# Small changes around four places where TensorE waits, in a one-core gated-attention kernel

## The chip, the core and the metric

The kernel runs on one core of a Trainium2 chip. The core has five engines that run side by side and wait for one another by semaphores: TensorE (PE in the profile: matrix products; PEld is its loading of weights), VectorE (DVE), ScalarE (ACT), GpSimd (POOL) and SyncE (SP, which here only issues transfers). Every float here is 32 bits wide; the products run on fp32r operands.

The metric is the device time of one execution in microseconds (us), as the median of some runs. The changed kernel is measured in the same way against the kernel before.

## The reference

`x` has 2,048 rows of 640 values. There are 32 heads of 128 values, each with its own keys and values, and a window of the last 512 of 2,048 cached positions; the dense branch has 1,728 hidden values.

```python
W = min(4096, max(256, Sk // 4))                  # 512
xn = (x - mean(x)) / sqrt(var(x) + 1e-5)          # per row

q = heads(xn @ wq)
scores = q @ k[:, -W:].T * Dh ** -0.5
o = softmax(scores) @ v[:, -W:]
s = merge(o) @ wo

h = relu(xn @ w1 + b1)
y = (h * h) @ w2 + b2
out = x + s * (y * sigmoid(y))
```

## The kernel before

Nearly everything is a product on TensorE, and precision is kept by splitting: each operand is written as a high part `hi` (a rounded copy, made by ScalarE) and a low part `lo = value - hi` (made by VectorE or GpSimd), and `triple` issues three matmuls, hi·hi, hi·lo and lo·hi, in this order. One matmul is 128x128 weights against 512 columns. The rows of `x` are cut into four tiles of 512 rows, t = 0 to 3, and the kernel works with values transposed (features on the partitions).

The program has three stages, one behind the other on TensorE.

1. **First steps (0 to 108 us).** Tile 0 is normalised and its dense branch is computed, 14 steps of an "up" product (`up`, w1, tile name `ph`) and a "down" product (`down`, w2, `py`). Beside it VectorE prepares the mean and the inverse deviation of the tiles 1 and 2 (T1, T2): `ln_load` reads the rows, `ln_block` takes the statistics into a tile `mv`, `ln_root` makes the inverse root. `mv` has a row on each partition, but what is needed is one value per column. So `ln_rows` turns `mv` (128 partitions x 8 values) round with a transposing matmul into a PSUM bank (`pmv`), copies it to a tile `lr`, stores that in DRAM (`mv_d`) and reads it back spread over all partitions (`mr`). `ln_chunk` then normalises the transposed `x` with it (`xc`).
2. **The other tiles' dense branch (108 to 284 us).** The up products of T1 and T2 are done together for pairs of weight blocks, with seven products in place of eight (`w_first` to `w_third`; a Strassen-Winograd form). For each pair p the kernel makes sums of weight blocks (`w_sums`, tiles `ws`), splits them into hi and lo (`w_split(p, 0)` gives `wa`, `w_split(p, 1)` gives `ws`, `w_split(p, 2)` gives `wc` and `wl`), and adds products on VectorE: in `w_second` the sum `wy = wa + p5`, in `w_third` the sum `wx = wa + p5`. PSUM banks are few, so a product into the bank of `wa` must wait until such a sum has read it. Between these, `gate(0, ...)` finishes tile 0. Then 28 "down" steps m follow (`c_load` reads, `c_prep` splits into `ch` and `cw` two steps ahead, `c_down` multiplies), and `gate(T1, ...)` after step 13 applies the sigmoid, which on ScalarE needs another function table. Tile 3 (LATE) gets its statistics in stage 2 with the same `ln_rows`, ahead of the last pair.
3. **Attention (284 to 1,949 us).** 128 units i, one head on one tile each, of 54 matmuls: `s_mm` (scores, `s`), `q_mm` (queries of a unit two ahead, `pq`), `v_mm` (`o`) and `r_mm` (output projection, `r`). In the first units early up products of tile 3 (`early_up`, `eu`) fill the places that the later stages don't use yet. Queries use one PSUM bank: `q_hi` (ScalarE) and `q_lo` (VectorE) must read it before the next `q_mm` may write it.

In stages 1 and 2 the code's own order counts: the wrapper `Ordered` keeps what `pe`, `dve`, `act`, `pool` and `sp` issue in program order on each engine, while calls through `nc.` are placed by the scheduler. In stage 3 the order comes from a list: `at(when, f, ...)` gives each call a planned time in us from the stage's start (a unit is `PERIOD` = 12.4 of these), and the calls are issued sorted by it. `pe.addr_align` puts empty instructions between units so that code blocks of 256 instructions end at chosen places.

Constants lie in the pool `cpool` (`ident`, `b_sb` with 96 floats a partition, four tiles `SQ` of 32 floats a partition), which stands ahead of all pools of the left side. In the built program every tile of 512 bytes or more per partition starts at a multiple of 512 bytes, but for one of the constants; two calls of `pad` with 480 bytes see to that on the right side.

Of the kernel before, what the change touches and what calls it, by code (L numbers as in the profile page):

```python
# [8 lines left out]
F32 = mybir.dt.float32  # L9
F32R = mybir.dt.float32r  # L10
AF = mybir.ActivationFunctionType
# [3 lines left out]
P = 128  # L15
NT = 512
# [9 lines left out]
def kernel(  # L26
# [14 lines left out]
    nc = tc.nc  # L41
# [4 lines left out]
    NB = NT // P  # L46
# [3 lines left out]
    LATE = NTILE - 1  # L50
# [89 lines left out]
    LS = {}  # L140

    def ln_load(t):
        mv = xp.tile([P, 4, NB], F32, tag="mv", name=f"mv{t}")[:, :2, :]
        sc = xp.tile([P, 3, NB], F32, tag="sc", name=f"sc{t}")
        xn = []
        for b in range(NB):
            xb = ln_tile(t, b)
            r0 = t * NT + b * P
            nc.sync.dma_start(xb, x[r0 : r0 + P, :])
            xn.append(xb)  # L150
        LS[t] = mv, sc, xn

    def ln_block(t, b):
        mv, sc, xn = LS[t]
        st = xp.tile([P, 2, 6], F32, tag="st", name=f"st{t}_{b}", bufs=4)
        hd = D // 2
        for i in range(2):
            dve.bn_stats(st[:, i, :], xn[b][:, i * hd : (i + 1) * hd])
        dve.bn_aggr(mv[:, :, b], st)

    def ln_var(t):
        mv, sc, xn = LS[t]
# [12 lines left out]
        return mv  # L175

    def ln_rows(t, mv):
        pm = psx.tile([P, NT], F32, tag="x", name=f"pmv{t}")
        (pe if t == LATE else nc.tensor).transpose(pm[: 2 * NB, :P], mv.rearrange("p a b -> p (a b)"), ident)
        row = xp.tile([2 * NB, P], F32, tag="lr", name=f"lr{t}", bufs=1)  # L180
        nc.vector.tensor_copy(row, pm[: 2 * NB, :P])
        d = dpool.tile([2, NT], F32, name=f"mv_d{t}")
        nc.sync.dma_start(d.rearrange("a (b p) -> (a b) p", p=P), row)
        bc = []
        for i in range(2):
            m = (
                pa.tile([P, D], F32, tag="xb", name=f"mr{t}_{i}", bufs=NB)
                if t == T2
                else xp.tile([P, D], F32, tag="mr", name=f"mr{t}_{i}")
            )[:, :NT]  # L190
            nc.sync.dma_start(m, d[i : i + 1, :].to_broadcast([P, NT]))
            bc.append(m)
        return bc
# [53 lines left out]
        return [PRE[0, k] for k in range(2)]  # L247

    def ln_first():
        mv = xp.tile([P, 4, NB], F32, tag="mv", name="mv0")  # L250
        sc = xp.tile([P, 3, NB], F32, tag="sc", name="sc0")
        sts = [xp.tile([P, 2, 6], F32, tag="st", name=f"st0_{b}", bufs=4) for b in range(NB)]
        n = NB // 2
# [428 lines left out]
        b["p5"] = xp.tile([P, NT], F32, tag="p5", name=f"p5_{p}", bufs=2)  # L682
        act.activation(b["p5"], b["y"], AF.Copy)

    def w_second(p):
        b = PB[p]
        prod(p, 6, b["a"])
        dve.tensor_tensor(b["y"], b["a"], b["p5"], op=ALU.add)
        prod(p, 2, b["x"])
        rest(p, 0, 0, b["x"])  # L690
        up_end(T1, PAIRS[p][0], b["x"])
# [127 lines left out]
    B32 = 32  # L819
# [407 lines left out]
    up(T2, rp)  # L1227
    w_load(2)
    w_sums(1)
    w_split(1, 0)  # L1230
    w_fifth(0)
    w_second(0)
    gate(0, gate_tile, (3, 4))
    w_split(1, 1)
    w_split(1, 2)
    NP = len(PAIRS)
    for p in range(1, NP):
        more = p + 1 < NP
        if p + 2 < NP:
            w_load(p + 2)  # L1240
        w_first(p)
        w_seed(p)

        def prepare():
            if more:
                w_split(p + 1, 0)
                w_sums(p + 1)
            else:
                for k in range(2):
                    c_prep(0, k)  # L1250

        w_third(p - 1, prepare, lambda: w_fifth(p))
        if p == 1:
            ln_load(LATE)
        if p in (2, 3):
            spill(p - 1, XS[p - 1])
        if 1 <= p <= NB:
            ln_block(LATE, p - 1)
        if p == NB:
            ln_var(LATE)  # L1260
            LN[LATE] = ln_root(LATE)
        if p == NP - 2:
            for m in range(3):
                c_load(m)
        if p == NP - 1:
            LN[LATE] = ln_rows(LATE, LN[LATE])
        w_second(p)
        if more:
            w_split(p + 1, 1)
            w_split(p + 1, 2)  # L1270
    up(T2, FC - 1)
    w_third(NP - 1, lambda: c_prep(1, 0), lambda: c_prep(1, 1))
    xctx.close()
    bctx.close()
    for m in range(2 * FC):
        t, f = CS[m]
        for n in {OPEN + 2: (m + 3, m + 4), OPEN + 3: ()}.get(m, (m + 3,)):
            if n < 2 * FC:
                c_load(n)
        if m + 2 < 2 * FC:  # L1280
            for k in range(2):
                c_prep(m + 2, k)
        c, odd = divmod(m - 2, 2)
        if not odd:
            if 0 <= c < DC:
                ln_chunk(LATE, c)
                for k in range(2):
                    ln_split(LATE, c, k)
            if 0 < c <= DC:
                spill(LATE, XS[LATE], slice(c - 1, c))  # L1290
        if m == OPEN:
            pools["ep"] = ctx.enter_context(tc.tile_pool(name="early", bufs=1, side="right"))
            load_raw("q", 0, 0)
            load_raw("k", 0, 0)
            open_xT(0, 0)
            for i in range(2):
                load_xT(0, 0, i, slice(0, DC))
        if m == OPEN + 2:
            for kind in "qk":
                prep(kind, 0, 0, dve)  # L1300
                load_raw(kind, 0, 1)
            open_xT(0, 1)
            for i in range(2):
                load_xT(0, 1, i, slice(0, DC))
        if m == OPEN + 4:
            for kind in "qk":
                prep(kind, 0, 1, dve)
        if m == 2 * FC - 1:
            hctx.close()
            pools["psa"] = ctx.enter_context(  # L1310
                tc.tile_pool(name="psa", bufs=1, space=PSUM, side="right")
            )
            q_mm(0, range(DC))
            q_hi(0)
            q_lo(0)
        if m in LEAD_STEPS:
            pe.addr_align(BLOCK, lead_slot(m))
        c_down(m)
        if m == FC - 1:
            gate(T1, gate_tile)  # L1320
# [69 lines left out]
    for i in range(NU):  # L1390
        t0 = i * PERIOD

        def on(when, f, *a):
            at(t0 + when, f, *a)

        hf, g, t, h = units[i]
        for c in range(KC):
            on(0.68 * c, align, i, SLOTS[c])
            on(0.68 * c, s_mm, i, c)
        on(0.68 * KC - 0.6, align, i, SLOTS[KC])  # L1400
        qs = [(i + AHEAD, 3.45 if i % G and i > UPG else 4.3, 4.1)]
        if i == 0:
            qs = [(1, 2.8, 4.1), (2, 9.1, PERIOD - 5.2)]
        elif i < UPG:
            qs = [(i + 2, 4.9 if i == 3 else 4.2, 4.1)]
        for n, q_at, low in qs if i + AHEAD < NU else ():
            for c in range(DC):
                on(q_at + 0.68 * c, q_mm, n, (c,))
            on(q_at + 3.5, q_hi, n)
            on(q_at + low, q_lo, n)  # L1410
        for c in range(KC):
            on(0.8 + 0.68 * c, max_fold, i, c)
        on(3.95, gather, i, "m")
        on(4.1, row, i, "m")
        for c in range(KC):
            on(10.4 + 0.4 * c, shift, i, c)
        on(11.7, expo, i, 0)
        on(12.7, p_hi, i, 0)
        on(13.8, expo, i, 1)
        on(PERIOD + 4.0, p_hi, i, 1)  # L1420
        on(13.9, p_lo, i, 0)
        on(16.2, s_add, i)
        on(PERIOD + 6.2, s_fold, i)
        on(PERIOD + 8.0, gather, i, "s")
        on(PERIOD + 8.5, row, i, "s")
        on(18.6, p_lo, i, 1)
        for c in range(KC):
            on(PERIOD + 8.5 + 0.68 * c, v_mm, i, c)
        on(2 * PERIOD + 4.2, o_norm, i)
        on(2 * PERIOD + 4.9, o_hi, i)  # L1430
        on(2 * PERIOD + 5.5, o_lo, i)
        if i % G == G - 1:
            for d in range(DC):
                last = i == NU - G - 1
                if i < NU - 1:
                    for when, js in (R_AT_END if last else R_AT)[d]:
                        on(when, r_mm, i, d, js, (R_BANK_END if last else R_BANK)[d])
                    on(when + 0.68 * len(js), r_acc, i, d)
                if g == NG - 1 and hf == 0:
                    at((i + (3, 4, 5, 4, 5)[d] + (t and d in (0, 3, 4))) * PERIOD + 4.3, store_acc, t, d)  # L1440
                    w = (NU // 2 + 9 + 4 * (t * DC + d)) * PERIOD
                    for k, n in enumerate("sxg"):
                        at(w + k * PERIOD - 0.6, load_finish, n, 0, t, d)
                    at(w + 3 * PERIOD - 0.7, finish_gate, 0, t, d)
                    at(w + 3 * PERIOD - 0.7, finish, 0, t, d)
# [67 lines left out]
    at(z + 32.0, late_h)  # L1513
    for n, ((f, c), u) in enumerate(zip(EARLY, EARLY_IN)):
        if u >= 0:
            first = EARLY_IN[n - 2] < u or u == 3
            at(
                u * PERIOD + (6.3 if u == 0 else 3.4 if first else 8.2) + 0.01 * n,
                early_up,
# [63 lines left out]
```

## Time and profile before

| what | value |
|---|---|
| median of 3 runs | 1951.23 us (1951.10 to 1951.89) |
| the profiled execution's own time | 1951.11 us |
| its span, first to last instruction | 1949.3 us |
| TensorE | busy 1941.4 us, 8,576 matmuls |
| VectorE | busy 1599.3 us |
| ScalarE | busy 1242.6 us |
| GpSimd | busy 1346.5 us |
| mean granted TensorE clock | 1.000 |

Rows of a timeline read: start, duration, engine, line, operation, output<-inputs, shape, count; a bracket at the end says how long the engine was idle before it and who ended that. Nearly all rows have line 77, that of the recording wrapper, so work is told apart by tile names; the profile leaves buffer numbers out. A matmul's row shows when it starts and when its last result is out, 0.39 us later for one alone, and the next one starts before that; so the time a group takes on TensorE is read from its start to the next group's start, not from its duration. Idle time of VectorE, ScalarE or GpSimd costs nothing unless TensorE ends up waiting for it.

### The profile page before, as it was taken

What the parts mean: (1) busy time and instruction counts of PE and PEld (TensorE: products, weight loads), DVE (VectorE), ACT (ScalarE), POOL (GpSimd) and SP (SyncE); (2) the same over time, 40 slices, a digit from 0 to 9 for tenths busy, and PEclk for the clock granted to TensorE, in tenths of its full rate; (3) what the DMA queues carried; (4) which work ended last, traced back from release to release, by engine and by line L of the source; (5) the groups of instructions that cost most, each with busy time, mean ns of one, the idle gap of its engine ahead of it and who ended that gap; (6) DMA issues with size and microseconds to landing.
All of it is one profiled execution on the core that took longest, in us unless ns stands there. A gap on an engine that the chain in (4) does not pass through costs nothing.

```text
span 1949.3 us, 28584 instructions
## 1 busy us (share of the span) xinstructions
PE 1941.4 (100%) x8576; PEld 1605.5 (82%) x8576; DVE 1599.3 (82%) x2758; ACT 1242.6 (64%) x2150; POOL 1346.5 (69%) x727
## 2 busy tenths in 40 slices
PE   9999999999999999999999999999999999999998
PEld 7888888888888888888888888888888888888887
DVE  6864747788888888888888878888888888888864
ACT  5665536766666666666666676666666666666643
POOL 0022107888888888888888878888888888888841
PEclk9999999999999999999999999999999999999999
DMA  7557953323233222332335433333333333332353
GB/s 221 184 192 252 366 190 109 95 88 96 90 92 95 91 91 93 92 92 92 93 100 184 140 109 109 114 114 115 114 114 114 114 114 114 97 93 92 85 187 119
DMA packets 147639, 246.43 MB, mean 126 GB/s; under 512 B 25020, under 2 KB 47334, under 8 KB 146214
## 3 DMA queue, kind: packets, MB, share of 16 engines
q1 hardware_dynamic: 144774, 232.64, 38.5%
q0 software_dynamic: 2576, 11.80, 1.5%
q8 instruction: 77, 1.26, 0.2%
q14 instruction: 68, 0.56, 0.1%
q10 hardware_dynamic: 144, 0.16, 0.0%
HBM read 213.59 MB, written 30.95 MB: 125 GB/s over the span
## 4 chain that ended last, share of the span: by engine, by line
PE 99%; DMA 0%; DVE 0%; SPq 0%; issue 0%; ACT 0%
PE pq L77 22%; PE r L77 22%; PE o L77 18%; PE s L77 18%; PE py L77 7%; PE ph L77 3%; PE ly L77 2%; PE wa L77 2%; PE lu L77 2%; PE wy L77 1%; PE wx L77 1%; PE eu L77 1%; DMA xb<-in_x_dram 0%; DMA wr<-in_w_dram 0%; PE px L77 0%; SPq L77 0%
## 5 line engine op out<-in xcount | busy, mean ns | idle before, releaser
L77 POOL TENSOR_TENSOR pt<-e,pt 128x1024 fp32r<-128x1024 f32 x256 | 615.2, 2403 | 113.5 <-ACT pt L77 68.9
L77 PE MATMUL r<-ot,wo 128*128 128x512 f32 x1920 | 496.6, 389 | 0.0
L77 PE MATMUL pq<-ax,wq 128*128 128x512 f32 x1920 | 456.1, 389 | 0.0
L77 PEld LDWEIGHTS pq<-ax,wq 128*128 128x128 f32 x1920 | 360.4, 188 | 75.1 <-DVE q L77 0.4
L77 PEld LDWEIGHTS r<-ot,wo 128*128 128x128 f32 x1920 | 360.5, 188 | 74.8
L77 PE MATMUL o<-pt,wv 128*128 128x512 f32 x1536 | 369.0, 389 | 0.0
L77 PE MATMUL s<-q,wk 128*128 128x512 f32 x1536 | 368.9, 389 | 0.0
L77 DVE TRANSPOSE_TENSOR_REDUCE rdm<-s 128x16 f32<-128x512 f32 x512 | 346.9, 712 | 8.0 <-PE s L77 7.9
L77 ACT ACTIVATE e<-e 128x1024 f32<-128x1024 f32 x256 | 269.7, 1054 | 123.3 <-DVE e L77 83.2
L77 PEld LDWEIGHTS s<-q,wk 128*128 128x128 f32 x1536 | 288.4, 188 | 59.8
L77 PEld LDWEIGHTS o<-pt,wv 128*128 128x128 f32 x1536 | 288.3, 188 | 59.9 <-POOL pt L77 0.2
L77 DVE TENSOR_TENSOR e<-s,bm 128x512 f32<-128x512 f32 x512 | 312.3, 665 | 5.3 <-DMA bm<-m_d 4.3
L77 POOL TENSOR_TENSOR su<-e,e 128x1024 f32<-128x1024 f32 x128 | 308.8, 2412 | 0.0
L77 ACT ACTIVATE pt<-e 128x1024 fp32r<-128x1024 f32 x256 | 272.0, 1062 | 6.9
L77 DVE TENSOR_TENSOR acc<-r,acc 128x512 f32<-128x512 f32 x300 | 203.6, 679 | 12.7 <-PE r L77 12.4
L77 ACT ACTIVATE rdm<-rdm 32x64 f32<-32x64 f32 x384 | 97.7, 255 | 182.3 <-DVE rdm L77 179.2
L77 DVE TENSOR_TENSOR ot<-o,ot 128x512 fp32r<-128x512 f32 x128 | 88.6, 692 | 86.1 <-ACT ot L77 86.1
L77 DVE TRANSPOSE_TENSOR_REDUCE rds<-su 128x32 f32<-128x1024 f32 x128 | 158.3, 1237 | 0.3 <-POOL su L77 0.3
L77 ACT ACTIVATE q<-pq 128x512 fp32r<-128x512 f32 x128 | 76.8, 600 | 120.0 <-PE pq L77 120.0
L77 ACT ACTIVATE rds<-rds 32x32 f32<-32x32 f32 x384 | 89.7, 234 | 60.0 <-DVE rds L77 56.6
L77 POOL TENSOR_TENSOR wo<-or,wo 128x640 fp32r<-128x640 f32 x64 | 101.0, 1578 | 30.1 <-ACT wo L77 30.1
L77 POOL TENSOR_TENSOR wv<-vr,wv 128x512 fp32r<-128x512 f32 x64 | 83.2, 1300 | 53.6 <-ACT wv L77 53.6
(171 smaller groups left out, 2005.3 us busy)
## 6 DMA issues: line engine op xcount, KB each, us to landing
bm<-m_d SPq DMA_DIRECT2D x128, 256.0 KB, 3.2
bs<-s_d SPq DMA_DIRECT2D x128, 256.0 KB, 4.0
qr<-in_wq_dram SPq DMA_DIRECT2D x64, 320.0 KB, 4.7
or<-in_wo_dram SPq DMA_DIRECT2D x64, 320.0 KB, 4.6
kr<-in_kT_dram SPq DMA_DIRECT2D x64, 256.0 KB, 4.4
vr<-in_v_dram SPq DMA_DIRECT2D x64, 256.0 KB, 4.4
cw<-in_w_dram SPq DMA_DIRECT2D x26, 320.0 KB, 4.5
h_m<-r SPq DMA_DIRECT2D x26, 256.0 KB, 2.1
```

What stands on the lines that cost most here:

```text
L77: ins = method(*args, **kwargs)
```

## The change

Five edits:

- `ln_rows` turns `mv` round on VectorE: `mv` grows to 32 values a partition (the unused ones set to zero by GpSimd), and one VectorE transposition in blocks of 32x32 writes `lr`. This gives the 8 rows in four pieces of 32 columns, so `mv_d` is written with four transfers in place of one. Three transposing matmuls, three PSUM tiles and three copies go. For T2 VectorE's transposition and SP's transfers also come earlier in their queues, ahead of the loads of w1 and w2 for step 9.
- At step m = 6 ScalarE runs a sigmoid over one value, into a new tile `table` (one float a partition, in `cpool`).
- In unit 1 all four early up products stand ahead of the queries of unit 3 (`pq3`), which move from 4.2 to 5.6 of the unit, and `q_lo` from 4.1 to 6.4 behind them.
- The split of the second pair's `wa` comes behind the fifth product's copy (`p5`) and the sum `wy` of the first pair.
- The splits of the second pair's `ws`, `wc` and `wl` come behind the first pair's sum `wx`.

```diff
     def ln_load(t):
-        mv = xp.tile([P, 4, NB], F32, tag="mv", name=f"mv{t}")[:, :2, :]
+        mv = xp.tile([P, 32 // NB, NB], F32, tag="mv", name=f"mv{t}")
+        nc.gpsimd.memset(mv[:, 2:, :], 0.0)
...
     def ln_rows(t, mv):
-        pm = psx.tile([P, NT], F32, tag="x", name=f"pmv{t}")
-        (pe if t == LATE else nc.tensor).transpose(pm[: 2 * NB, :P], mv.rearrange("p a b -> p (a b)"), ident)
-        row = xp.tile([2 * NB, P], F32, tag="lr", name=f"lr{t}", bufs=1)
-        nc.vector.tensor_copy(row, pm[: 2 * NB, :P])
+        row = xp.tile([P, B32], F32, tag="lr", name=f"lr{t}", bufs=1)
+        nc.vector.transpose(row, mv.rearrange("p a b -> p (a b)"))
         d = dpool.tile([2, NT], F32, name=f"mv_d{t}")
-        nc.sync.dma_start(d.rearrange("a (b p) -> (a b) p", p=P), row)
+        to = d.rearrange("a (b p) -> (a b) p", p=P)
+        for g in range(0, P, B32):
+            nc.sync.dma_start(to[:, g : g + B32], row[g : g + 2 * NB, :])
...
-    def w_second(p):
+    def w_second(p, between=None):
         b = PB[p]
         prod(p, 6, b["a"])
         dve.tensor_tensor(b["y"], b["a"], b["p5"], op=ALU.add)
+        if between:
+            between()
         prod(p, 2, b["x"])
...
     w_sums(1)
-    w_split(1, 0)
     w_fifth(0)
-    w_second(0)
+    w_second(0, lambda: w_split(1, 0))
     gate(0, gate_tile, (3, 4))
-    w_split(1, 1)
-    w_split(1, 2)
...
         def prepare():
+            if p == 1:
+                w_split(1, 1)
+                w_split(1, 2)
             if more:
...
+    table = cpool.tile([P, 1], F32, name="table")
     for m in range(2 * FC):
         t, f = CS[m]
+        if m == 6:
+            act.activation(table, b2_sb[:, :1], AF.Sigmoid)
...
         elif i < UPG:
-            qs = [(i + 2, 4.9 if i == 3 else 4.2, 4.1)]
+            qs = [(i + 2, {1: 5.6, 3: 4.9}.get(i, 4.2), 6.4 if i == 1 else 4.1)]
...
-            first = EARLY_IN[n - 2] < u or u == 3
+            first = EARLY_IN[n - 2] < u or u in (1, 3)
```

The order of the built program shows it at three places. The first is VectorE's queue between the first two pairs of stage 2 (`ws1`, `wa1`, `wc1`, `wl1` belong to the second pair, the sums `wy0` and `wx0` to the first; a name ending in `_1_` and a number on the left is a lo part). Before:

```order
L77 TENSOR_TENSOR ws1_1_1277<-wp1_0_1124,ws1_0_1276 128x256
L77 TENSOR_TENSOR wa1_1_1283<-wp1_0_1124,wa1_0_1282 128x512
L77 TENSOR_TENSOR wy0_1248<-wa0_1241,p5_0_1292 128x512
L77 SCALAR_TENSOR_TENSOR sg_1314<-py0_3_368,b_sb_65,sg_1314 128x512
L77 SCALAR_TENSOR_TENSOR sg_1318<-py0_4_369,b_sb_65,sg_1318 128x512
L77 TENSOR_TENSOR ws1_1_1323<-ws1_0_1276,ws1_0_1322 128x512
L77 TENSOR_TENSOR ws1_1_1323<-ws1_1_1277,ws1_0_1322 128x512
L77 TENSOR_TENSOR wc1_1_1329<-wp1_1_1126,wc1_0_1328 128x256
L77 TENSOR_TENSOR wl1_1_1331<-wp1_0_1124,wl1_0_1330 128x128
L77 TENSOR_TENSOR wl1_1_1331<-wp1_1_1126,wl1_0_1330 128x128
L77 TENSOR_TENSOR wx0_1249<-wa0_1241,p5_0_1292 128x512
```

And after:

```order
L77 TENSOR_TENSOR ws1_1_1281<-wp1_0_1128,ws1_0_1280 128x256
L77 TENSOR_TENSOR wy0_1252<-wa0_1245,p5_0_1292 128x512
L77 TENSOR_TENSOR wa1_1_1302<-wp1_0_1128,wa1_0_1301 128x512
L77 SCALAR_TENSOR_TENSOR sg_1318<-py0_3_369,b_sb_65,sg_1318 128x512
L77 SCALAR_TENSOR_TENSOR sg_1322<-py0_4_370,b_sb_65,sg_1322 128x512
L77 TENSOR_TENSOR wx0_1253<-wa0_1245,p5_0_1292 128x512
L77 TENSOR_TENSOR ws1_1_1348<-ws1_0_1280,ws1_0_1347 128x512
L77 TENSOR_TENSOR ws1_1_1348<-ws1_1_1281,ws1_0_1347 128x512
L77 TENSOR_TENSOR wc1_1_1354<-wp1_1_1130,wc1_0_1353 128x256
```

The lo part of `wa1` has moved one place back, behind the sum `wy0`, and the sum `wx0` has moved ahead of the five lo parts of the second pair. On ScalarE the same two moves stand: the copy `p5` is ahead of the hi part of `wa1`, and the copy `wx1<-wa1` ahead of the hi parts of `ws1`, `wc1` and `wl1`.

The second place is ScalarE's queue in the "down" steps (`ch` and `cw` with a step's number are hi parts, `xT3` is a hi part of tile 3). Step 6 before:

```order
L77 ACTIVATE cw7_0_2142<-cw7_2098 128x640
L77 ACTIVATE ch8_0_2166<-ch8_2136 128x512
L77 ACTIVATE cw8_0_2170<-cw8_2134 128x640
L77 ACTIVATE xT3_0_2053<-xc3_2_2174 128x512
L77 ACTIVATE ch9_0_2202<-ch9_2164 128x512
```

Step 6 after; ahead of T1's gate (`sg<-py1`), where the `ACT_TABLE_LOAD` stood before, there is none any more, and the number of table loads stays at six:

```order
L77 ACTIVATE cw7_0_2149<-cw7_2105 128x640
L77 ACT_TABLE_LOAD
L77 ACTIVATE table_1987<-b_sb_65 128x1
L77 ACTIVATE ch8_0_2174<-ch8_2143 128x512
L77 ACTIVATE cw8_0_2178<-cw8_2141 128x640
L77 ACTIVATE xT3_0_2060<-xc3_2_2182 128x512
```

A table load and the one-value sigmoid have come between the hi parts of steps 7 and 8.

The third place is TensorE's queue in unit 1. The end of the early products and the start of the queries before:

```order
L77 MATMUL eu12_3056<-xT3_1_2054,w1s12_960 128x512
L77 MATMUL eu12_3056<-xT3_0_2053,w1s12_960 128x512
L77 MATMUL pq3_3075<-ax0_1_0_2722,wq0_1_0_2772 128x512
L77 MATMUL pq3_3075<-ax0_1_1_2723,wq0_1_0_2772 128x512
L77 MATMUL pq3_3075<-ax0_1_0_2722,wq0_1_1_2773 128x512
```

And after, with six more matmuls of `eu12` ahead; before, these six stood behind the fifteen of `pq3`:

```order
L77 MATMUL eu12_3064<-xT3_1_2061,w1s12_964 128x512
L77 MATMUL eu12_3064<-xT3_0_2060,w1s12_964 128x512 x2
L77 MATMUL eu12_3064<-xT3_1_2061,w1s12_964 128x512
L77 MATMUL eu12_3064<-xT3_0_2060,w1s12_964 128x512 x2
L77 MATMUL eu12_3064<-xT3_1_2061,w1s12_964 128x512
L77 MATMUL eu12_3064<-xT3_0_2060,w1s12_964 128x512
L77 MATMUL pq3_3092<-ax0_1_0_2730,wq0_1_0_2780 128x512
L77 MATMUL pq3_3092<-ax0_1_1_2731,wq0_1_0_2780 128x512
```

The queries of unit 3 now start six matmuls later and end where the early products ended.

Last, the tile `table` lengthens the pool of the constants by 32 bytes a partition, and `mv` and `lr` change the length of the pool that holds them. In the built program most tiles of the left side (the accumulators, `ot`, the attention tiles `e`, `pt`, `bm`, and all of stages 1 and 2 but what lies on the right) now start 32, 160 or 288 bytes behind a multiple of 512. Of the 8,573 matmuls left, 4,791 read at least one operand that starts 32 bytes off a multiple of 64; before there was none.

More of the change, by code (lines that the diff above doesn't have):

```diff
@@ L158, in ln_block @@
             dve.bn_stats(st[:, i, :], xn[b][:, i * hd : (i + 1) * hd])
-        dve.bn_aggr(mv[:, :, b], st)
+        dve.bn_aggr(mv[:, :2, b], st)
     def ln_var(t):
@@ L249, in ln_first @@
     def ln_first():
-        mv = xp.tile([P, 4, NB], F32, tag="mv", name="mv0")
+        mv = xp.tile([P, 32 // NB, NB], F32, tag="mv", name="mv0")
         sc = xp.tile([P, 3, NB], F32, tag="sc", name="sc0")
```

## The prediction

> **What bounds the kernel now.** I read the page first, for the busy times.
>
> ```profile
> span 1949.3 us, 28584 instructions
> PE 1941.4 (100%) x8576; PEld 1605.5 (82%) x8576; DVE 1599.3 (82%) x2758; ACT 1242.6 (64%) x2150; POOL 1346.5 (69%) x727
> ```
>
> TensorE is idle for 1949.3 - 1941.4 = 7.9 us in all, and no other engine comes near it. A faster engine beside it gains nothing by itself; only matmuls that go, or places where TensorE waits, can gain. So the next view is the chain in order of time, for the pace and for what breaks it.
>
> ```profile
> 190.54 46.47 PE py L77 x205
> 237.04 43.40 PE py L77 x190
> 280.44 3.40 PE pq L77 x15
> ```
>
> The first row gives 46.47 / 205 = 0.2267 us from matmul to matmul: 15 take 3.40 us, 6 take 1.36 us. The 395 matmuls of the first two rows should take 89.53 us and take 280.44 - 190.54 = 89.90, 0.37 us more, all of it at the seam between the two. I then went through TensorE's timeline for every group that takes longer than its count allows. Where the change edits, I find seven; each is priced below as the start of the next group, minus its own start, minus count x 0.2267.
>
> **The transposes.** The first two, for T1 and T2:
>
> ```profile
> 40.31 0.27 PE L179 MATMUL pmv<-ident,mv 128*8 128x128 f32 x1
> 40.34 3.65 PE L77 MATMUL ph<-xT,w1s 128*128 128x512 f32 x15
> 43.83 3.56 PE L77 MATMUL py<-h,w2s 128*128 128x512 f32 x15
> ...
> 54.03 0.27 PE L179 MATMUL pmv<-ident,mv 128*8 128x128 f32 x1
> 54.06 3.67 PE L77 MATMUL ph<-xT,w1s 128*128 128x512 f32 x15
> 57.57 3.56 PE L77 MATMUL py<-h,w2s 128*128 128x512 f32 x15
> ```
>
> 43.83 - 40.31 - 3.40 = 0.12 us, and 57.57 - 54.03 - 3.40 = 0.14 us. The third (LATE) I take at their mean: 0.39 us in all, which goes. What comes instead must stay hidden. For T1:
>
> ```profile
> 40.94 0.30 SPq L183 DMA_DIRECT2D mv_d<-lr  x1
> 42.18 0.80 SPq L191 DMA_DIRECT2D mr<-mv_d  x2
> ...
> mr<-mv_d SPq DMA_DIRECT2D x6, 256.0 KB, 4.4
> ...
> 50.93 1.41 DVE L77 TENSOR_TENSOR xc<-xc,mr 128x512 f32<-128x512 f32 x2
> ```
>
> Three more stores of 0.30 us each put 0.90 us ahead of the two reads and of the weight loads queued behind them on SP. The reads then start at 43.1 and land by 43.1 + 0.8 + 4.4 = 48.3, 2.6 us before `xc` uses them; VectorE in turn no longer waits for TensorE's `pmv`. For T2 and LATE SP reaches the stores earlier in its queue, before the loads of step 9 and between stores of `h_m`; 0.9 us again, with a whole step of 6.80 us (two groups of 15) before the steps that use those loads. GpSimd's three memsets stand where it has nothing else to do until stage 2. I cost all of this at 0; if the cover were gone, each place would cost at most its 0.9 us.
>
> **The sigmoid.** ScalarE and VectorE at that seam:
>
> ```profile
> 233.46 0.74 ACT L77 ACTIVATE cw<-cw 128x640 fp32r<-128x640 f32 x1 [2.14 <-issue]
> 234.22 1.28 ACT L77 ACT_TABLE_LOAD   x1
> 235.51 3.00 ACT L77 ACTIVATE sg<-py,b_sb 128x512 f32<-128x512 f32 x5
> ...
> 236.24 3.39 DVE L77 SCALAR_TENSOR_TENSOR sg<-py,b_sb,sg 128x512 f32<-128x512 f32 x5 [1.18 <-ACT sg L77]
> ```
>
> T2's first "down" product needs a PSUM bank that VectorE has finished reading, at 236.24 + 3.39 / 5 = 236.92; TensorE goes on at 237.04, and needs two more matmuls to find its pace. The bank's own sums are complete 12 matmuls before the step's end, at about 234.3, when ScalarE is done with `cw`; without the 1.28 us table load `sg` starts there, over a microsecond earlier, and the bank is free at about 235.8, ahead of TensorE. The 0.37 us goes, and nothing is late behind it, since the four other banks follow at 0.68 us (3.39 / 5), the pace of three matmuls. The load itself moves to step 6:
>
> ```profile
> 209.06 0.61 ACT L77 ACTIVATE ch<-ch 128x512 fp32r<-128x512 f32 x1
> ...
> 212.76 0.63 ACT L77 ACTIVATE xT<-xc 128x512 fp32r<-128x512 f32 x1 [2.36 <-DVE xc L77]
> ```
>
> It delays `ch8` and `cw8` (209.06 on) by some 1.5 us, and through VectorE's queue the next `xT`. Step 8 starts on TensorE after 115 matmuls, at 190.54 + 26.1 = 216.6. Now ScalarE is through with `ch8` at 209.7, and three more operations of 0.6 to 0.8 us follow on the two engines (211.9 at the latest), so some 3 us are left after the delay. Cost 0. SP's order changes there as well (a read of attention's `ax` ahead of those of step 13, which starts only at 190.54 + 12 x 3.40 + 2.27 = 233.6); cost 0, and rival (d) below if not.
>
> **The fourth Q.**
>
> ```profile
> 305.44 1.52 PE L77 MATMUL eu<-xT,w1s 128*128 128x512 f32 x6
> 306.99 3.70 PE L77 MATMUL pq<-ax,wq 128*128 128x512 f32 x15
> 310.52 1.52 PE L77 MATMUL eu<-xT,w1s 128*128 128x512 f32 x6
> ...
> 306.28 0.65 DVE L77 SCALAR_TENSOR_TENSOR q<-pq,q 128x512 fp32r<-128x512 f32 x1
> ```
>
> 310.52 - 305.44 = 5.08 us for 21 matmuls of 4.76 us: 0.32 us, because the query bank is free only when VectorE's `q` ends at 306.93. Six early products in between take 1.36 us, so `pq3` starts at 308.16, 1.2 us after the bank is free. 0.32 us goes. What could be late next is the other side: `pq3` now ends at 311.6, so its hi part comes after ScalarE's other preparations, and its lo part behind four shifts on VectorE:
>
> ```profile
> 312.81 2.43 DVE L77 TENSOR_TENSOR e<-s,bm 128x512 f32<-128x512 f32 x4
> ...
> 318.68 3.56 PE L77 MATMUL pq<-ax,wq 128*128 128x512 f32 x15
> ```
>
> The lo part thus ends at about 312.81 + 2.43 + 0.65 = 315.9, and the bank is asked for again at 318.68 - 0.32 = 318.4. 2.5 us are left; cost 0.
>
> **The second pair's splits.** Here the edit moves work in both directions.
>
> ```profile
> 117.44 0.61 ACT L77 ACTIVATE wa<-wp 128x512 fp32r<-128x512 f32 x1
> 118.08 0.60 ACT L77 ACTIVATE p<-wy 128x512 f32<-128x512 f32 x1
> ...
> 117.82 1.26 DVE L77 TENSOR_TENSOR ws<-wp,ws 128x256 f32<-128x256 f32 x1
> 119.00 0.68 DVE L77 TENSOR_TENSOR wa<-wp,wa 128x512 fp32r<-128x512 f32 x1
> 119.61 0.69 DVE L77 TENSOR_TENSOR wy<-wa,p 128x512 f32<-128x512 f32 x1
> ...
> 124.77 0.70 DVE L77 TENSOR_TENSOR wx<-wa,p 128x512 f32<-128x512 f32 x1
> ...
> 119.33 1.60 PE L77 MATMUL wa<-xT,wa 128*128 128x512 f32 x6
> 120.77 1.54 PE L77 MATMUL wa<-T,ws 128*128 128x512 f32 x6
> ...
> 124.19 1.52 PE L77 MATMUL wy<-T,ws 128*128 128x512 f32 x6
> 125.55 1.62 PE L77 MATMUL wa<-T,wc 128*128 128x512 f32 x6
> 127.01 0.84 PE L77 MATMUL wa<-xT,wl 128*128 128x512 f32 x3
> ```
>
> The fourth product's group takes 127.01 - 125.55 - 1.36 = 0.10 us too long: its bank waits for the sum `wx` (124.77 to 125.47). With that sum ahead of the lo parts it is done by about 123.7, and the 0.10 us goes. But the first product of pair 1 (119.33) already takes 120.77 - 119.33 - 1.36 = 0.08 us too long. Its third matmul, due at 119.78, needs the lo part of `wa1`, which ends at 119.68 and reaches TensorE hardly in time. After the change VectorE makes `wy` first, whose inputs are ready (`p` on ScalarE by 118.1), at 119.00; so the lo part starts at 119.61 and ends 0.61 us later than now, with nothing in between to take this up. The wait grows by 0.61 us. The bounds: -0.08 us if the lo part comes in time after all (the `ws` row of 1.26 us may be shorter in another execution), +1.30 us if one more operation like the sum `wy` (0.69 us) gets ahead of it. I take 0.61, which stands on the rows at that very place. The lo parts of `ws1` come later as well (ready by 124.4, needed by the third matmul of the group at 124.19 + 0.61, that is at 125.3): cost 0.
>
> **The sum.** -0.39 - 0.37 - 0.32 - 0.10 + 0.61 = -0.57 us. The profiled execution took 1951.11 us in all, so 1950.54; it lies 0.12 us under the median of the runs, 1951.23, against which the sum gives 1950.7. That is 0.03% less. A measurement of this kernel can tell about 0.2%, 3.9 us, from no change; so this is no change.
>
> **Where the tiles lie.** The 32 bytes of `table` move most tiles of the left side off multiples of 512 bytes. The trace of before has no such operand, so it has no price for it. What it can hit first is the start, where nothing hides a transfer:
>
> ```profile
> 0.75 1.81 SPq L77 DMA_DIRECT2D xb<-in_x_dram  x4
> 3.63 0.89 DVE L77 BATCH_NORM_STATS2 st<-xb 128x6 f32<-128x320 f32 x2 [2.58 <-DMA xb<-in_x_dram]
> ```
>
> From issue to use are 2.88 us. Between 0 and, say, an eighth of this (0.36 us) I take 0, because no row shows a cost; the upper end stays in the range. [...] Later transfers have the margins above.
>
> **Rivals.** (a) Engines read the moved tiles slower, and the kernel is slower. 4,791 of the 8,573 matmuls read a moved operand. This decides at 3.9 + 0.6 = 4.5 us, which is 0.94 ns a matmul, 0.4% of 226.7 ns. At 1 ns the time would be 1950.7 + 4.8 = 1955.5, at 3 ns 1965. For it: there is not one such matmul before. Against it: the pace of all groups is the same 0.2267 us, whatever the operands. Chance 7%. [...]
> (b) The edits don't do what they say: the freed places are taken by a next wait a little later (the sigmoid's banks, the query bank), only the transposes' 0.39 us goes, and `wa1` costs its 0.61: 1951.23 + 0.22 = 1951.5. Chance 15%.
> (c) The `wa1` wait doesn't come, all gains do: 1951.23 - 1.18 - 0.08 = 1950.0. Chance 14%.
> (d) A new wait of one to three microseconds at a place that I hold covered (stores ahead of loads on SP, `ax` ahead of step 13's operands): 1952 to 1954. Chance 8%.
> (e) Faster by over 3.9 us: it would need half of TensorE's 7.9 us of idle time, and the places that the edits touch hold 1.3 us in all, the transposes included. Chance 1%.
>
> The forecast itself has the other 55%: between 1950.3 and 1951.2. The range, 1949.8 to 1952.8, holds the forecast, (b), (c) and part of (d), and the 0.36 us of the start. Within 0.2% are the forecast, (b), (c) and (d): 92%; slower 7%; faster 1%.
>
> **What would show it.** In the changed profile there should be 8,573 matmuls, no `pmv`; the `ph` groups of steps 5 and 7 should follow their `py` without an extra 0.1 us. The 395 `py` should take 89.5 us. `pq3` should start right behind twelve `eu` and take 3.40 us to the next group. The first product of pair 1 should take about 2.05 us to the next group, with VectorE's lo part of `wa` ending at its third matmul. A group of 15 that lasts more than 3.41 us in stage 3 would show rival (a); an idle row of TensorE that ends at a DMA, rival (d).

## The result: 1.7% slower, nearly all of it in the pace of the matmuls

The changed kernel takes 1984.67 us (median of 4 runs, 1984.42 to 1985.26), the kernel before on the same chip 1951.56 us: a ratio of 1.017 [1.0157, 1.0182], 33.1 us more. The prediction said 1950.7 and at most 1952.8.

The page of the profile after, first lines:

```profile
span 1982.9 us, 28597 instructions
PE 1973.9 (100%) x8573; PEld 1604.6 (81%) x8573; DVE 1615.9 (81%) x2758; ACT 1244.8 (63%) x2151; POOL 1348.2 (68%) x730
```

TensorE does three matmuls fewer and is busy 32.5 us longer (1941.4 before); its idle time has grown by 1.1 us only (from 7.9 to 9.0). So new waits do not explain the time. The granted clock is 1.00 in both. The page's costliest groups tell where the 32.5 us are. Before:

```profile
L77 PE MATMUL r<-ot,wo 128*128 128x512 f32 x1920 | 496.6, 389 | 0.0
L77 PE MATMUL pq<-ax,wq 128*128 128x512 f32 x1920 | 456.1, 389 | 0.0
L77 PE MATMUL o<-pt,wv 128*128 128x512 f32 x1536 | 369.0, 389 | 0.0
L77 PE MATMUL s<-q,wk 128*128 128x512 f32 x1536 | 368.9, 389 | 0.0
```

After:

```profile
L77 PE MATMUL r<-ot,wo 128*128 128x512 f32 x1920 | 509.6, 396 | 0.0
L77 PE MATMUL pq<-ax,wq 128*128 128x512 f32 x1920 | 459.1, 390 | 0.0
L77 PE MATMUL o<-pt,wv 128*128 128x512 f32 x1536 | 379.0, 395 | 0.0
L77 PE MATMUL s<-q,wk 128*128 128x512 f32 x1536 | 373.7, 392 | 0.0
```

The first number behind the bar is the group's busy time, the second the mean duration of one matmul. The four groups of attention take 13.0 + 3.0 + 10.0 + 4.8 = 30.8 us more. Nothing waits longer there; each matmul is a little slower, and the groups are not equally slow. The timeline of TensorE in the steady part of attention, three rows of before and then the stretch after the change:

```profile
1007.57 2.88 PE L77 MATMUL o<-pt,wv 128*128 128x512 f32 x12
1010.28 1.52 PE L77 MATMUL r<-ot,wo 128*128 128x512 f32 x6
1011.64 1.52 PE L77 MATMUL s<-q,wk 128*128 128x512 f32 x6
```

```profile
1000.95 1.56 PE L77 MATMUL r<-ot,wo 128*128 128x512 f32 x6
1002.35 2.92 PE L77 MATMUL s<-q,wk 128*128 128x512 f32 x12
1005.11 0.86 PE L77 MATMUL r<-ot,wo 128*128 128x512 f32 x3
1005.81 3.59 PE L77 MATMUL pq<-ax,wq 128*128 128x512 f32 x15
1009.24 1.56 PE L77 MATMUL r<-ot,wo 128*128 128x512 f32 x6
```

Six r take 1002.35 - 1000.95 = 1.40 us, that is 233.3 ns each; before they took 1011.64 - 1010.28 = 1.36 us, 226.7 ns each. Fifteen pq take 3.43 us in place of 3.40. Taken over all matmuls of the trace, from start to next start, the mean went from 226.7 ns to 233.6 for r, 233.3 for o, 229.8 for s and 228.3 for pq.

Which groups are slow agrees with where their operands lie. For r and o the moving operand (`ot`, `pt`) has moved by 32 bytes and the weights (`wo`, `wv`, on the right side) have not; both are at 233. In stage 2, wx<-xT,wa has moved weights and an unmoved moving operand, and is at 233.3. But py<-h,w2s, where both operands have moved, is at 226.8 as before. Of the 8,516 large matmuls (those of 512 columns), 3,813 now have operands whose start places differ when taken modulo 256 bytes; before there was none. The groups s and pq have not moved at all and lose their time in the first five to eight matmuls behind an r or o.

### The profile page after: what moved, and what is told of

Its sections match the earlier page's. It is cut to its first block, busy times and chain, and to the rows that moved or that the text cites. A ratio compares the mean times of both kernels' runs of the same rounds, so it can differ in the third digit from the quotient of the medians.

```text
span 1982.9 us, 28597 instructions
## 1 busy us (share of the span) xinstructions
PE 1973.9 (100%) x8573; PEld 1604.6 (81%) x8573; DVE 1615.9 (81%) x2758; ACT 1244.8 (63%) x2151; POOL 1348.2 (68%) x730
## 3 DMA queue, kind: packets, MB, share of 16 engines
q1 hardware_dynamic: 144918, 232.65, 37.2%
## 4 chain that ended last, share of the span: by engine, by line
PE 98%; DVE 1%; ACT 0%; DMA 0%; issue 0%; SPq 0%; DVEq 0%
PE r L77 23%; PE pq L77 22%; PE o L77 18%; PE s L77 18%; PE py L77 7%; PE ly L77 2%; PE ph L77 2%; PE wa L77 2%; PE lu L77 2%; PE wy L77 1%; PE wx L77 1%; PE eu L77 1%; DVE T L77 0%; DVE ws L77 0%; DVE ts L77 0%; DMA wr<-in_w_dram 0%
## 5 line engine op out<-in xcount | busy, mean ns | idle before, releaser
L77 PE MATMUL r<-ot,wo 128*128 128x512 f32 x1920 | 509.6, 396 | 0.0
L77 PE MATMUL o<-pt,wv 128*128 128x512 f32 x1536 | 379.0, 395 | 0.0
L77 PE MATMUL s<-q,wk 128*128 128x512 f32 x1536 | 373.7, 392 | 0.0
L77 DVE TRANSPOSE_TENSOR_REDUCE rdm<-s 128x16 f32<-128x512 f32 x512 | 353.9, 716 | 10.5 <-PE s L77 10.1
```

Source lines behind the costliest of these rows:

```text
L77: ins = method(*args, **kwargs)
```

## The experiments

Theories first, by the letters that the expectations use. Q: the moved work costs the time (new waits, queues). O: every operand off its place costs by itself. M: what counts is that the two operands of a matmul start at different places, taken modulo some number of bytes. V: VectorE, ScalarE and GpSimd are slower on moved tiles, and TensorE suffers from that. A time below without a number of runs is that of one run; the runs of one kernel on one chip lie within 2.2 us of each other here.

**All five edits, tiles put back.** The changed kernel with the 32 bytes taken off another constant's tile, whose last floats nothing uses. All large products but 30 then have operands that agree modulo 256 bytes again; those 30, of `ph`, have weights 128 bytes off:

```diff
-    b_sb = cpool.tile([P, 96], F32, name="b_sb")
+    b_sb = cpool.tile([P, 88], F32, name="b_sb")
```

> The changed kernel with the tile of constants b_sb shortened from 96 to 88 floats a partition, which takes back the 32 bytes of table: every matmul operand starts at a multiple of 64 bytes again; all five edits stay. Theory M (a matmul is slow, by 6.7 to 7.0 ns, where its moving operand and its weights start at different places modulo 64 bytes): 226.7 ns from matmul to matmul everywhere, and only the five edits' own sum is left, 1951.6 - 0.6 = 1951.0 us. Theory O (any operand off a multiple of 64 is slow): the same 1951.0. Theory Q (the edits' own waits on TensorE leave it in a slow pace, the places of the tiles don't matter): 1984 to 1985.

Measured: 1950.55 us (11 runs) against 1951.56, a ratio of 0.9995 [0.9986, 1.0004]. The 33 us are gone although every edit is still there. Q falls.

**The 32 bytes alone.** The kernel before with that tile longer by 8 floats, and no other edit:

```diff
-    b_sb = cpool.tile([P, 96], F32, name="b_sb")
+    b_sb = cpool.tile([P, 104], F32, name="b_sb")
```

> The kernel before with b_sb lengthened from 96 to 104 floats, 32 bytes a partition, and nothing else: the left side's tiles move by 32 bytes as in the changed kernel, none of the five edits is there. Theories M and O: as slow as the changed kernel and 0.6 us more, since the edits' gain is missing: 1985.2 us. Theory Q: 1951.6.

Measured: 1985.18 us. The shift alone makes the whole slowdown.

**The same with 64 bytes** (112 floats).

> The kernel before with b_sb lengthened by 64 bytes: the left side's tiles move off their multiples of 512, but stay at multiples of 64. Theory M with a period of 64 bytes, and O: 1951.6 us, no change. If the multiple of 512 counts, or of 128: as slow as with 32 bytes, 1985 us. Theory Q: 1951.6.

Measured: 1978.36 us, 26.8 more than before. M with a period of 64 bytes falls, and so does O with multiples of 64: 64 bytes are not a harmless distance. The branch that foresaw the slowness of 32 bytes misses too, since this kernel is 6.8 us faster than that one. The timeline of this kernel:

```profile
1000.16 2.93 PE L77 MATMUL s<-q,wk 128*128 128x512 f32 x12
1002.93 0.86 PE L77 MATMUL r<-ot,wo 128*128 128x512 f32 x3
1003.63 3.61 PE L77 MATMUL pq<-ax,wq 128*128 128x512 f32 x15
1007.08 1.55 PE L77 MATMUL r<-ot,wo 128*128 128x512 f32 x6
1008.47 2.91 PE L77 MATMUL o<-pt,wv 128*128 128x512 f32 x12
1011.22 1.08 PE L77 MATMUL r<-ot,wo 128*128 128x512 f32 x4
```

Twelve o, with operands 64 bytes apart, take 2.75 us, 229 ns each, and twelve s, with both operands in place, 2.77 us, 231 ns each. The matmuls behind a change from one kind of group to the other settle slowly: the s at 1000.16 follow each other at 234, 231, 233, 236, 224, 231, 236, 228, 232, 231 ns and only then at 227.

**Only one operand of one group.** The kernel before, with the attention outputs 32 bytes later in slots that have room behind them:

```diff
-        OT[i] = [two[:, k, :NT] for k in range(2)]
+        OT[i] = [two[:, k, 8 : 8 + NT] for k in range(2)]
```

> The kernel before with the two halves of ot used from their 8th float on (32 bytes further inside the same tile), which moves the moving operand of the 1,920 r matmuls alone. Theories M and O: r goes from 226.7 to about 233.6 ns, 13.4 us, and the matmuls behind an r group (s, pq) take part of the 7.8 us that they lost in the changed kernel, 3 to 4: 1965 to 1969 us; o stays at 226.7. Theory Q: 1951.6.

Measured: 1974.17 us, 22.6 more. The mechanism is as expected, the size is not: r takes 13.2 us more (509.8 us busy), and the unmoved s, o and pq, at 228.2 to 228.6 ns, take the rest, 8.9 us. I had put 3 to 4 us on s and pq and nothing on o.

**Everything off, but equally.** This tells M from O and V: the changed kernel with an unused tile of 224 bytes at the top of the right side, which puts that side at 32 bytes too.

```diff
+    top = ctx.enter_context(tc.tile_pool(name="top", bufs=1, side="right"))
+    top.tile([P, 56], F32, name="top")
     xr = xctx.enter_context(tc.tile_pool(name="mxr", bufs=1, side="right"))
```

> The changed kernel with every tile of the right side moved by 32 bytes too, so that in all but 30 of the large products both operands start 32 bytes behind a multiple of 256. Theory M (what counts is the difference between the start places of the moving operand and of the weights, taken modulo 256 bytes): all groups go back to 226.7 ns a matmul, time 1950.5 to 1951. Theory O (every operand that does not start at a multiple of 256 bytes costs by itself): now all 8,573 matmuls have two such operands, time 1985 or more. Theory V (other engines are slower on moved tiles, and TensorE suffers from that): 1985 or more as well, since no tile of theirs has come back.

Measured: 1951.31 us (10 runs) against 1951.83, a ratio of 0.9997 [0.9988, 1.0007]. The page's groups of this kernel:

```profile
L77 PE MATMUL r<-ot,wo 128*128 128x512 f32 x1920 | 496.6, 389 | 0.0
L77 PE MATMUL pq<-ax,wq 128*128 128x512 f32 x1920 | 456.0, 389 | 0.0
L77 PE MATMUL o<-pt,wv 128*128 128x512 f32 x1536 | 369.3, 389 | 0.1
L77 PE MATMUL s<-q,wk 128*128 128x512 f32 x1536 | 369.1, 389 | 0.0
```

All groups are back at 389 ns, with 8,486 matmuls that read two operands off their places, and VectorE, ScalarE and GpSimd still working on moved tiles. O and V fall, M stands. VectorE's busy time says the same: it is 1615.9 us in the changed kernel and 1597.2 here, so it follows TensorE's pace and does not set it.

**The period and the grain.** The one line of `ot` again, with 1, 4, 16, 32, 48 and 64 floats in place of 8.

> The kernel before with the two halves of each attention output tile starting at the 2nd float of their slots, 4 bytes later; it is the moving operand of 1,920 products r. Theory M, with every difference counted in bytes: r at about 233 ns a matmul and the products behind it slower for some steps, as with 32 bytes, time 1965 to 1975. Theory M with a grain of 16 or 32 bytes: 4 bytes don't count, time 1951.5, r at 226.7 ns.

> The kernel before with the attention output tiles 16 bytes later in their slots. If the pace falls off with the difference of the two start places (236.0 ns at 4 bytes, 233.8 at 32), r takes 234 to 236 ns a matmul and the time is 1974 to 1985. [...]

> The same with 64 bytes: r at 229 to 231 ns (o had 228.9 and r 231.1 where both stood 64 bytes off their weights), 1,920 x 2.3 to 4.4 ns plus some steps of the products behind, time 1956 to 1965. If only the distance to the next multiple of 256 counted in one direction, falling from 4 to 128 bytes, r would be between 232.0 and 233.8 ns, time 1968 to 1974.

> The same with 128 bytes (the 33rd float). Theory M with a period of 256 bytes: r at about 231.7 ns, the mean of the few products of other kernels here whose operands differ by 128 bytes; 1,920 x 5.0 ns = 9.6 us and some steps of the products behind, time 1961 to 1970. With a period of 128 bytes: 1951.5, r at 226.7 ns.

> The same with 192 bytes, that is 64 bytes ahead of the next multiple of 256. If the sign of the difference counts (products with weights 64 bytes behind the moving operand took 233.4 ns, with the moving operand 64 bytes behind the weights 228.9), r is at 233 to 234 ns, time 1970 to 1976. If only its size counts, r is as with 64 bytes.

> The same with 256 bytes (the 65th float). Theory M with a period of 256 bytes: r at 226.7 ns, time 1951.5. With a period of 512 bytes or none: r slower than 228 ns, time 1960 or more.

Measured, with the mean of r from start to next start, and the range of the three other groups' means:

| `ot` later by | time, us | over before | r, ns | s, o, pq, ns |
|---|---|---|---|---|
| 4 bytes | 1985.40 | +33.6 | 236.0 | 229.3 to 230.2 |
| 16 bytes | 1972.36 | +20.4 | 231.2 | 228.6 to 229.7 |
| 32 bytes | 1974.17 | +22.6 | 233.8 | 228.2 to 228.6 |
| 64 bytes | 1980.45 | +28.5 | 232.2 | 229.9 to 230.7 |
| 128 bytes | 1968.43 | +16.6 | 232.0 | 227.9 to 228.3 |
| 192 bytes | 1971.27 | +19.3 | 233.3 | 227.9 to 228.3 |
| 256 bytes | 1951.32 | -0.5 | 226.7 | 226.7 |

The view of the instructions of `r` shows the two ends: shortest, median and longest duration in ns. With 4 bytes, and with 256:

```profile
L77 PE MATMUL r<-ot,wo x1920: 395/398/405, 337.6 to 1917.7; 128*128 128x512 f32 x192
```

```profile
L77 PE MATMUL r<-ot,wo x1920: 389/389/397, 337.1 to 1883.7; 128*128 128x512 f32 x192
```

The period is 256 bytes: 256 bytes cost nothing (-0.5 us), 128 do (16.6 us). No distance tried between 4 and 192 bytes is free, and the loss does not fall or rise with the distance. Three expectations missed. At 4 bytes I expected r at about 233 ns and at most 1975 us; it is the dearest distance, with 236.0 ns and 1985.40 us. At 16 bytes I weighed a fall of the pace with the distance, with r at 234 to 236 ns; it is at 231.2, faster than at 32 bytes. Below 16 bytes only 4 were run, so no grain is shown. At 64 bytes I expected r at 229 to 231 ns and at most 1965 us; r is at 232.2, and the settling of s, o and pq (3 to 4 ns on each of 4,992 matmuls) made it 1980.

The 192 bytes came out as expected, with r at 233.3 ns. With 64 bytes and with 192, which is 64 ahead of the next multiple of 256, the same kernel loses 28.5 and 19.3 us: the sign of the difference does count.

**Own weights, or the next ones?** While a matmul runs, the weights of the next one are loaded: in the trace of before a load lasts 188 ns and starts 0.22 us ahead of its own matmul, when the matmul before it has just started. N: the columns of the running matmul collide with that load. S: a matmul's columns stand against its own weights. The lo halves of `ot` and of `wo` are moved by 4 bytes, both and each alone:

```diff
-        OT[i] = [two[:, k, :NT] for k in range(2)]
+        OT[i] = [two[:, k, k : k + NT] for k in range(2)]
...
+        if tag == "wo":
+            o = name.startswith("wo")
+            two = [
+                pools["eo"].tile([P, D + 64 * i], F32R, tag=f"wo{i}", name=f"{name}_{i}", bufs=bufs)
+                for i in range(2)
+            ]
+            return [two[0], two[1][:, o : o + D]]
```

> The kernel before with the lo half of each attention output (ot) and the lo half of wo both 4 bytes later, the hi halves in place. A triple is hi with hi, lo with hi, hi with lo (ot first). Theory N (what collides is the reading of a product's columns and the loading of the next product's weights): the lo half of ot streams while the lo half of wo is loaded, both 4 bytes off, and the hi halves stream while hi halves are loaded, so every pair agrees: time 1951.5, r at 226.7 ns. Theory S (what counts is a product's columns against its own weights): two of the three products of each triple differ by 4 bytes, 1,280 in all; with 236.0 ns for them and slow steps in the other groups the time is 1968 to 1985.

> Control: only the lo half of ot 4 bytes later. By N and by S alike one product of each triple differs, 640 in all, and the time is 1957 to 1975. If it stays at 1951.5, one product in three is too few to matter, and the run with both lo halves moved cannot tell N from S by its time.

> Second control: only the lo half of wo 4 bytes later. By N the second product of a triple (the lo half of ot streams in place while the moved lo half of wo is loaded) collides, by S the third; either way 640 in all, and 1957 to 1975.

Measured: 1971.38, 1964.30 and 1970.97 us, against 1951.26 before. N as stated falls: with both halves moved every moving operand agrees with the weights loaded beside it, and 20.1 us are lost. The times lie where S has them. But S is not the whole of it: two differing products in three (20.1 us) cost no more than the one with `wo` alone (19.7), and in that run the second product of a group, whose own operands agree, already takes 235 ns on average, while the moved weights of the third are loaded. N and S at once would order the three times: they hit the second and third product of a triple in the first run, the second alone in the second run, and the second and third again in the last one. But the third product of a group takes only 228 ns there, so this is not shown either. Which two accesses collide stays open. The weight loads themselves last 188 ns in all these runs, as before.

**The edits without one of them.** The first experiment's kernel, with the split of the second pair's `wa` back where it was:

```diff
-    w_fifth(0)
-    w_second(0, lambda: w_split(1, 0))
+    w_split(1, 0)
+    w_fifth(0)
+    w_second(0)
```

> The changed kernel with all tiles back in place (as in the run with 88 floats in b_sb) and with the split of the second pair's wa back where it was before the change; the other edits stay. The wait at the first product of pair 1, 0.63 us in that run, should go back to the 0.08 us of before: 0.55 us less than that run, 1950.0, and 1.5 us under the kernel before. If the wait moves to the fourth product or to the sum wy, it stays at 1950.5.

Measured: 1950.05 us (11 runs) against 1951.97, a ratio of 0.9990 [0.9981, 0.9999]. It is the fastest kernel of this study, by a margin that is at the edge of what can be told. The product in question, in the first experiment's kernel and then in this one:

```profile
118.96 0.61 PE L77 MATMUL wa<-xT,wa 128*128 128x512 f32 x2
119.94 1.20 PE L77 MATMUL wa<-xT,wa 128*128 128x512 f32 x4 [0.36 <-DVE wa L77]
120.97 1.53 PE L77 MATMUL wa<-T,ws 128*128 128x512 f32 x6
```

```profile
119.11 1.56 PE L77 MATMUL wa<-xT,wa 128*128 128x512 f32 x6
120.51 1.53 PE L77 MATMUL wa<-T,ws 128*128 128x512 f32 x6
```

With the edit the six matmuls take 2.01 us, 0.65 over 1.36; without it 1.40.

## Why the prediction was wrong

**The step that failed** is "Where the tiles lie", and with it rival (a). I priced the new operand places at 0 for all but the start, gave rival (a) 7%, and held against it that "the pace of all groups is the same 0.2267 us, whatever the operands". That was no evidence: in the trace of before all 8,516 large matmuls had operands that agree modulo 256 bytes, so the one thing that the shift changes did not vary there. An equal pace over groups that are alike in this says nothing about groups that are not. The profile could not give the price, 30.8 us in attention; only a run could. The range should have reached for that rival, since nothing of before bounded it.

The rival's own form was wrong in three ways. It counted 4,791 matmuls that read a moved operand; what counts are the 3,813 whose two operands differ, and the 957 large ones whose operands lie off together keep the pace of before where they stand among themselves (py<-h,w2s, 226.8 ns). At 1 or 3 ns a matmul it was also priced too low: r alone has 6.9. And it left out the neighbours: s and pq, with no moved operand, lose 4.8 and 3.0 us of the 30.8. The sign that the prediction named for it did come: fifteen pq take 3.43 us in stage 3, over its 3.41.

The runs with `ot` alone moved show what a distance costs: 32 bytes cost r 7.1 ns a matmul, 16 bytes 4.5, and of the distances run only 256 bytes cost nothing. The measurement decides.

**The start.** The transfers into moved places were priced at 0 and bounded by 0.36 us, at the first block of x. No run shows that bound, an eighth of the 2.88 us from issue to use; in its place stand the times of the two profiles. That block comes no later: VectorE's first row with it starts at 3.59 us after, at 3.63 before. But the first large matmul starts at 12.17 us after, at 11.69 before:

```profile
11.69 1.63 PE L77 MATMUL ph<-xT,w1s 128*128 128x512 f32 x6
```

```profile
12.17 1.64 PE L77 MATMUL ph<-xT,w1s 128*128 128x512 f32 x6
```

These 0.48 us come from the third block, for which VectorE waits after, and did not before:

```profile
6.03 0.49 DVE L77 BATCH_NORM_STATS2 st<-xb 128x6 f32<-128x320 f32 x1
```

```profile
6.52 0.49 DVE L77 BATCH_NORM_STATS2 st<-xb 128x6 f32<-128x320 f32 x1 [0.54 <-DMA xb<-in_x_dram]
```

That the places cause this is not shown. The first large matmul starts at 11.77 to 12.17 us (12.02 on average) in the four kernels whose blocks of x lie 32, 64 or 160 bytes behind a multiple of 256: after, 32 and 64 bytes alone, everything off equally. It starts at 11.55 to 11.97 (11.73 on average) in the eleven with blocks at a multiple of 256. The averages differ by 0.3 us, within the bound, and the ranges overlap; the 0.48 us of the two executions above lie over it. In the first experiment and in the kernel with `wa` back the blocks lie 128 bytes behind such a multiple, and the matmul starts at 11.54 and 11.67, among the earliest. So in these two executions a start 128 bytes off a multiple of 256 did not make the matmul late.

Later transfers are not visibly slower: the main queue's packets take 37.2% of 16 engines' 1982.9 us, less than the 38.5% of 1949.3 us before.

**The five edits.** The sum was -0.57 us. The first experiment, where they stand alone, measures -1.0 us with an interval of -2.7 to +0.8, which cannot settle it; the rows of its trace can:

| term | predicted | in the first experiment |
|---|---|---|
| three transposes | -0.39 | -0.36: 3.41, 3.40 and 1.37 us to the next group in place of 3.52, 3.54 and 1.48 |
| sigmoid | -0.37 | gone: no step over 227 ns at that seam |
| fourth Q | -0.32 | gone: twelve eu in 2.72 us, fifteen pq in 3.40 |
| fourth product | -0.10 | gone: 1.36 us |
| `wa1` | +0.61 | 0.65 in place of 0.08: +0.57 |

The sums agree within 0.1 us. The 30 `ph` products with operands 128 bytes apart, which take 232.3 ns each, add 0.17 us that belong to the places and not to the edits. And the kernel with the split of `wa` back in its place loses the `wa1` term as worked out: 0.04 us too long where it was 0.65. The seam of the sigmoid is seen in the changed kernel's chain too; before, the 395 matmuls took 89.90 us:

```profile
192.69 89.54 PE py L77 x395
```

No new wait of rival (d)'s size came, and none of the freed places was taken by a next one, as rival (b) had it. (One group of twelve o is 0.17 us too long in the first experiment; in the kernel with `wa` back it is not.) Each of the prediction's five terms was right to a tenth of a microsecond. Their sum was worth 0.03% of the time; what the prediction could not see was worth 1.7%.

## What to carry to other kernels

On this chip, for products like these (fp32r, 128x128 weights, 512 columns; no others were run), keep the start of a matmul's moving operand and that of its weights at the same distance behind a multiple of 256 bytes. A common distance of 32 bytes was as good as none (1951.31 us against 1951.83). A small tile in a pool ahead of everything can break that for thousands of matmuls (3,813 here), so compare the tiles' addresses of both builds, not only the order of instructions. And a pace that is equal over all groups is evidence only for what differs between these groups.

## What was not expected of the hardware

- A matmul of 128x128 weights and 512 columns in fp32r follows the last one after 226.7 ns when its two operands, and those of the matmuls around it, agree modulo 256 bytes, and after 229 to 236 ns on average when they don't; 4 bytes are the worst distance tried (236.0 ns, 4% more).
- The loss outlasts its cause: behind such a group, matmuls with agreeing operands need up to ten steps, mostly of 224 to 236 ns, to come back to 226.7. With `ot` 64 bytes later, the page's groups are these:

```profile
L77 PE MATMUL r<-ot,wo 128*128 128x512 f32 x1920 | 507.2, 394 | 0.0
L77 PE MATMUL pq<-ax,wq 128*128 128x512 f32 x1920 | 462.2, 392 | 0.0
L77 PE MATMUL o<-pt,wv 128*128 128x512 f32 x1536 | 375.3, 393 | 0.0
L77 PE MATMUL s<-q,wk 128*128 128x512 f32 x1536 | 375.1, 393 | 0.0
```

  Of the 371 stretches of s, o or pq behind an r, 370 take ten steps there. The three unmoved groups lose 6.1 + 6.3 + 6.2 = 18.6 us against before, more than r itself (10.6).
- A weight load lasts 188 ns either way, and VectorE, ScalarE and GpSimd work as fast on tiles moved by 32 bytes as on others: busy 1597.2, 1242.8 and 1347.1 us with everything moved, 1599.3, 1242.6 and 1346.5 before.
